# Alternating two column tiles, matmul by matmul, in the weights-times-values product of the left-over rows, and lowering its planned cost

## The chip, the cores and the metric

The kernel runs on one core of one Trainium2 chip. The metric is device time in microseconds, of the slowest core (here the only one).

## The reference

Attention with a threshold, then a gated feed-forward layer:

```python
scores = scale * (q @ k.T)                       # 8 batches, 8 heads, 576 rows, head dim 64
thresh = scores.max(-1) - tau
attn   = softmax(where(scores >= thresh, scores, -1e9))
x      = (attn @ v)  -> [4608, 512]
xn     = x / rms(x) * rms_g
out    = (silu(xn @ w_gate) * (xn @ w_val)) @ w_out     # 512 -> 1536 -> 512
```

576 rows are 4 chunks of 128 and 64 rows left over. The kernel puts the 64 left-over rows of two batches into one chunk of 128 ("virtual" chunks, four of them). Since the two halves need different values v, their weights-times-values product cannot be one matmul on all 128 output rows; it runs on two column tiles of TensorE, 64 output rows each.

## The kernel before

The product, for two head pairs `i` per block. `kind == "v"` is a virtual chunk; its two `rows` are the two column tiles. 8 such blocks run in the kernel, 64 plain ones.

```python
def fn(o):
    for i in range(2):
        w, p = wt[(s - 1 + i) % NWT], p1 - 1 + i
        rows = [(slice(0, 128), b % 2)] if kind == "m" else [(HALF[e], e) for e in range(2)]
        for rs, vi in rows:
            at = 2 * i * (D + 1)
            nc.tensor.matmul(ring[...][rs, at:at + 2 * (D + 1)], w[:, 4, rs], va[vi][:, p, 8:10], start=True, stop=False)
            for h in range(2):
                for j in range(4):
                    nc.tensor.matmul(ring[...][rs, at:at + D + 1], w[:, 5 * h + j, rs], va[vi][:, p, 2 * j + h], ...)
                at += D + 1
```

The kernel does not issue its operations in the order in which the source names them. Each is recorded with a planned cost, and a planner then decides, with a model of engines and buffers, in which order all engines get their instructions:

```python
COST = dict(s_main=932.0, s_virt=900.0, ..., av_main=310.0, av_virt=480.0, ...)   # planned ns
...
o = add("PE", 2 * COST["av_main" if kind == "m" else "av_virt"], s + AV_PRIO, deps, fn, ring="R", mode=...)
...
seq = order_ops(ops, {"R": 4})       # 4 PSUM buffers, shared by transposes, products and feed-forward
for o in seq:
    o.fn(o)
```

Scores have PSUM buffers of their own, one per head of a pair (`s_ps`); VectorE reads them (line 592), and the next score step (line 569; its 16 or 8 matmuls are called a score block below) may overwrite a half only when that has been read.

## Time and profile before

| | before |
|---|---|
| median time, 3 runs | 563.74 us (563.67 to 563.99) |
| TensorE busy | 554.2 us, 99% |
| the 8 column-tile blocks, first to last start | 942 ns each, 7.5 us in all |
| TensorE waiting seen between instructions after 98.9 us | 0.6 us |

The profiled span is 561.9 us, about 1.8 us less than the time of an execution. The prediction shows the lines and says how they are read.

### The profile page before, as it was taken

What the parts mean: (1) busy time and instruction counts of PE and PEld (TensorE: products, weight loads), DVE (VectorE), ACT (ScalarE), POOL (GpSimd) and SP (SyncE); (2) the same over time, 40 slices, a digit from 0 to 9 for tenths busy, and PEclk for the clock granted to TensorE, in tenths of its full rate; (3) what the DMA queues carried; (4) which work ended last, traced back from release to release, by engine and by line L of the source; (5) the groups of instructions that cost most, each with busy time, mean ns of one, the idle gap of its engine ahead of it and who ended that gap; (6) DMA issues with size and microseconds to landing.
All of it is one profiled execution on the core that took longest, in us unless ns stands there. A gap on an engine that the chain in (4) does not pass through costs nothing.

```text
span 561.9 us, 15217 instructions
## 1 busy us (share of the span) xinstructions
PE 554.2 (99%) x5768; PEld 316.4 (56%) x5768; DVE 425.3 (76%) x1091; ACT 460.0 (82%) x741; POOL 322.4 (57%) x462
## 2 busy tenths in 40 slices
PE   8999999999999999999999999999999999999997
PEld 4756666757667455545555455545555444445674
DVE  4989977869968589658885889578966886586354
ACT  5999999998989788879888997888988988885332
POOL 2378846975767456665667666666666664551000
PEclk9999999999999999999999999999999999999999
DMA  9999999889976499889997799989998544652211
GB/s 200 271 291 250 173 179 216 161 143 198 195 181 115 116 174 160 185 156 183 154 176 175 121 170 176 182 177 156 174 189 179 110 97 97 151 95 53 85 38 38
DMA packets 270025, 89.08 MB, mean 159 GB/s; under 512 B 252544, under 2 KB 262272, under 8 KB 269952
## 3 DMA queue, kind: packets, MB, share of 16 engines
q1 hardware_dynamic: 267168, 86.02, 76.4%
q0 software_dynamic: 1600, 1.57, 1.7%
q8 instruction: 45, 0.74, 0.6%
q10 hardware_dynamic: 1184, 0.52, 0.3%
q14 instruction: 28, 0.23, 0.1%
HBM read 37.75 MB, written 9.44 MB: 84 GB/s over the span
## 4 chain that ended last, share of the span: by engine, by line
PE 95%; DVE 2%; POOL 1%; ACT 1%; issue 1%; DVEq 0%; POOLq 0%
PE s_ps L569 29%; PE ring L795 17%; PE ring L800 16%; PE ring L865 15%; PE ring L700 6%; PE ring L304 2%; PE ring L696 2%; DVE ssb L592 1%; PE ring L662 1%; PE ring L365 1%; PE s_ps L800 1%; PE s_ps L840 1%; PE s_ps L865 1%; PE s_ps L262 1%; PE s_ps L795 0%
## 5 line engine op out<-in xcount | busy, mean ns | idle before, releaser
L592 DVE CUSTOM_DVE_ANT_0 ssb<-s_ps,zrow 128x576 f32<-128x576 f32 x288 | 207.1, 753 | 64.3 <-PE s_ps L569 46.5
L610 ACT ACTIVATE ssb<-ssb,nth 128x576 f32<-128x576 f32 x224 | 166.1, 767 | 26.7 <-POOL nth L599 26.2
L569 PE MATMUL s_ps<-qkt 64*64 64x288 f32 (+1 forms) x1792 | 166.4, 417 | 1.5 <-DVE mx L592 1.5
L643 POOL TENSOR_SCALAR wsb<-ssb,nth 128x576 f16<-128x576 f32 x64 | 110.5, 1726 | 11.6 <-DMA wt<-wsb 6.3
L795 PE MATMUL ring<-xnT,wg 128*128 128x256 f16 (+1 forms) x564 | 114.4, 325 | 0.3 <-DVE xsb L718 0.3
L569 PEld LDWEIGHTS s_ps<-qkt 64*64 64x64 f32 (+1 forms) x1792 | 78.4, 140 | 62.8 <-DVE mx L592 15.5
L800 PE MATMUL ring<-xnT,wv 128*128 128x512 f16 (+1 forms) x528 | 110.4, 331 | 0.0
L599 POOL TENSOR_SCALAR nth<-mx 128x2 f32<-128x2 f32 x144 | 31.7, 220 | 128.6 <-DVE mx L592 114.4
L812 DVE SCALAR_TENSOR_TENSOR sl<-th,ring 128x256 f32<-128x256 f32 (+1 forms) x141 | 77.0, 546 | 30.5 <-ACT th L809 29.5
L617 ACT ACTIVATE wsb<-ssb 128x1152 f16<-128x1152 f32 x80 | 93.0, 1162 | 3.4 <-DMA wt<-wsb 1.1
L809 ACT ACTIVATE th<-ring 128x256 f32<-128x256 f32 (+1 forms) x141 | 67.7, 481 | 30.7 <-PE ring L795 26.6
L865 PE MATMUL ring<-wo,hf 128*128 128x512 f16 x384 | 90.0, 380 | 0.0
L648 POOL TENSOR_TENSOR wsb<-wsb,esb 128x576 f16<-128x576 f16 x64 | 81.8, 1279 | 10.1 <-ACT esb L629 5.7
L817 DVE TENSOR_TENSOR hf<-ring,sl 128x512 f16<-128x512 f32 (+1 forms) x132 | 75.0, 568 | 9.3 <-PE ring L800 0.5
L800 PEld LDWEIGHTS <-wv 128*128 128x128 f16 x576 | 52.2, 98 | 44.5 <-issue 14.2
L795 PEld LDWEIGHTS <-wg 128*128 128x128 f16 x576 | 52.0, 98 | 42.2 <-issue 12.2
L865 PEld LDWEIGHTS <-hf 128*128 128x128 f16 x408 | 37.3, 98 | 47.0 <-issue 7.0
L629 ACT ACTIVATE esb<-ssb,nth 128x576 f16<-128x576 f32 x64 | 49.2, 769 | 6.4 <-POOL nth L599 6.0
L700 PE MATMUL ring<-va,wt 128*128 128x65 f16 (+1 forms) x1264 | 52.9, 193 | 0.0
L700 PEld LDWEIGHTS <-wt 128*128 128x128 f16 (+1 forms) x1280 | 48.7, 100 | 3.8 <-issue 0.7
L614 ACT ACTIVATE wsb<-ssb 128x576 f16<-128x576 f32 x64 | 43.6, 681 | 1.6
L696 PE MATMUL ring<-va,wt 128*128 128x130 f16 (+1 forms) x158 | 35.1, 227 | 0.6 <-ACT qTv L473 0.6
(68 smaller groups left out, 444.8 us busy)
## 6 DMA issues: line engine op xcount, KB each, us to landing
vst<-in_v_dram SPq DMA_DIRECT2D x32, 256.0 KB, 3.8
qkn<-in_k_dram SPq DMA_DIRECT2D x31, 256.0 KB, 4.5
out_dram<-osb SPq DMA_DIRECT2D x31, 256.0 KB, 2.8
qkn<-in_q_dram SPq DMA_DIRECT2D x28, 256.0 KB, 4.2
stage<-in_moe_w_gate_dram SPq DMA_DIRECT2D x6, 512.0 KB, 6.1
stage<-in_moe_w_val_dram SPq DMA_DIRECT2D x6, 512.0 KB, 6.2
wt<-wsb SPq DMA_TRANSPOSE x128, 3.2
wo<-in_moe_w_out_dram POOLq DMA_DIRECT2D x4, 384.0 KB, 6.9
```

Source lines behind the costliest of these rows:

```text
L569: nc.tensor.matmul(s_ps[h][rows, ROW_AT + n * part:ROW_AT + n * part + n], lhs(hs), kT[i][p][h][hs, n * part:n * part + n], start=True, st ...
L592: nc.vector.tensor_tensor_reduce(out=ssb[a][:, h], in0=s_ps[h][:, ROW_AT:ROW_AT + S], in1=zrow, scale=-1.0 / 8.0, scalar=3.0e38, op0=ALU.a ...
L610: nc.scalar.activation(out=ssb[a][:, h], in_=ssb[a][:, h], func=PRELU, scale=-1.0, bias=nth[m][:, h:h + 1], **PRELU_KW)
L617: nc.scalar.activation(out=wsb[s % NW], in_=ssb[a], func=AF.Exp)
L643: nc.gpsimd.tensor_scalar(out=wsb[s % NW][:, h], in0=ssb[a][:, h], scalar1=nth[m][:, h:h + 1], scalar2=None, op0=ALU.is_le)
L648: nc.gpsimd.tensor_tensor(out=wsb[s % NW][:, h], in0=wsb[s % NW][:, h], in1=esb[es], op=ALU.mult)
L700: nc.tensor.matmul(ring[o.slot[0]][rs, at:at + D + 1], w[:, 5 * h + j, rs], va[vi][:, p, 2 * j + h], start=False, stop=(h == 1 and j == 3))
L795: nc.tensor.matmul(ring[o.slot[0]][:, 0:n], wg[d][:, fs], xnT[slot][:, d, 0:n], start=(d == 0), stop=(d == 3))
L800: nc.tensor.matmul(ring[o.slot[0]][:, 0:n], wv[d][:, fs], xnT[slot][:, d, 0:n], start=(d == 0), stop=(d == 3))
L812: nc.vector.scalar_tensor_tensor(out=sl[i][:, 0:n], in0=th[i][:, 0:n], scalar=1.0, in1=ring[g.slot[0]][:, 0:n], op0=ALU.add, op1=ALU.mult)
L817: nc.vector.tensor_tensor(out=hf[hi][:, 0:n], in0=ring[vv.slot[0]][:, 0:n], in1=sl[i][:, 0:n], op=ALU.mult)
L865: nc.tensor.matmul(ring[(first or o).slot[0]], hf[hs[fc][0]][:, 128 * j:128 * (j + 1)], wo[:, fc], start=(fc == 0), stop=(fc == NFC - 1))
```

## The change

The matmuls of the two column tiles alternate one by one, so that the two tiles can work at the same time. The planned cost of such a block is lowered with it.

```diff
-    ..., av_main=310.0, av_virt=480.0, ...
+    ..., av_main=310.0, av_virt=320.0, ...
@@
+                at = 2 * i * (D + 1)
                 for rs, vi in rows:
-
-                    at = 2 * i * (D + 1)
                     nc.tensor.matmul(... w[:, 4, rs], ... start=True, stop=False)
-                    for h in range(2):
-                        for j in range(4):
+                for h in range(2):
+                    for j in range(4):
+                        for rs, vi in rows:
                             nc.tensor.matmul(... w[:, 5 * h + j, rs], ... start=False, stop=(h == 1 and j == 3))
-                        at += D + 1
+                    at += D + 1
```

More of the change, by code (lines that the diff above doesn't have):

```diff
@@ L16 @@
 COST = dict(
-    s_main=932.0, s_virt=900.0, tr_qk=530.0, tr4=230.0, tr_full=440.0, av_main=310.0, av_virt=480.0, ffn4=216.0, warm=3500.0,
+    s_main=932.0, s_virt=900.0, tr_qk=530.0, tr4=230.0, tr_full=440.0, av_main=310.0, av_virt=320.0, ffn4=216.0, warm=3500.0,
     ttr=690.0, evac_qk=600.0, evac_half=380.0, evac_kt=350.0, prelu=700.0, exp2=1250.0, exp1=690.0, exp0=690.0,
```

## The prediction

> **What bounds the kernel now**
>
> I read five views, from coarse to fine. First the head of the page, its busy times and its chain of work that ended last.
>
> ```profile
> span 561.9 us, 15217 instructions
> PE 554.2 (99%) x5768; PEld 316.4 (56%) x5768; DVE 425.3 (76%) x1091; ACT 460.0 (82%) x741; POOL 322.4 (57%) x462
> PE 95%; DVE 2%; POOL 1%; ACT 1%; issue 1%; DVEq 0%; POOLq 0%
> ```
>
> TensorE is busy 99% of the span and holds 95% of the chain. Busy alone proves little, since overlapping matmuls count as one stretch, but the chain agrees: what shortens TensorE's own work shortens the kernel, unless something else has become the limit at that place.
>
> So I asked where that might be, with busy time by stretch. The first 98.9 us hold no instruction that the change touches. The columns are the stretch, its length, then busy us with instruction counts for PE, PEld, DVE, ACT and POOL, the granted clock, the DMA share and GB/s.
>
> ```profile
> 98.90:175.00 76.10, 75.53 (x905) 51.00 (x905) 60.83 (x176) 68.50 (x118) 54.51 (x73) 1.00 0.88 171
> 175.00:520.00 345.00, 345.00 (x3455) 177.96 (x3454) 265.09 (x641) 292.50 (x455) 207.67 (x284) 1.00 0.77 149
> ```
>
> From 175 to 520 us PE is busy 345.00 of 345.00. From 98.9 to 175 us it misses 0.57 us, ACT is at 90% and DMA at 88%. That stretch hides more waiting, because a wait between two halves of a score block lies under matmuls still in flight. The chain in order of time shows it (start, length, engine and line):
>
> ```profile
> 127.95 1.13 PE s_ps L569 x16
> ...
> 133.30 1.69 PE s_ps L569 x16
> ...
> 142.04 1.70 PE s_ps L569 x16
> ```
>
> A score block of 16 matmuls takes 1.13 us undisturbed; some here take 1.69. I compared every block and gap after 98.9 us with the median of its kind: about 2.9 us of excess lies between 98.9 and 175 us (0.73 us of it before the weights-times-values block at 173.55), and 0.27 us in all the rest. So there are two regimes: some slack up to 175 us, none afterwards.
>
> Now the operations themselves. The rows by form show which of the weights-times-values matmuls are touched: those in 128*64, on one column tile.
>
> ```profile
> L700 PE MATMUL ring<-va,wt 128*128 128x65 f16 x1008 | 44.4, 193 | 0.0
> L700 PE MATMUL ring<-va,wt 128*64 128x65 f16 x256 | 8.4, 195 | 0.0
> L696 PE MATMUL ring<-va,wt 128*64 128x130 f16 x32 | 7.1, 244 | 0.0
> ```
>
> There are 256 + 32 = 288 of them, in 8 blocks of 36: two head pairs, times two batches, times one 130-wide and eight 65-wide matmuls. Do not read their cost from 8.4 and 7.1: those spans overlap each other. Nor from 195 ns, which is the latency of one. What counts is start to start, which the timeline of the first block gives (start, length, line, form, count):
>
> ```profile
> 98.92 0.24 PE L696 MATMUL ring<-va,wt 128*64 128x130 f16 x1
> 99.00 0.32 PE L700 MATMUL ring<-va,wt 128*64 128x65 f16 x5
> 99.14 0.24 PE L696 MATMUL ring<-va,wt 128*64 128x130 f16 x1
> 99.16 0.38 PE L700 MATMUL ring<-va,wt 128*64 128x65 f16 x8
> 99.35 0.24 PE L696 MATMUL ring<-va,wt 128*64 128x130 f16 x1
> 99.37 0.38 PE L700 MATMUL ring<-va,wt 128*64 128x65 f16 x8
> 99.56 0.24 PE L696 MATMUL ring<-va,wt 128*64 128x130 f16 x1
> 99.59 0.47 PE L700 MATMUL ring<-va,wt 128*64 128x65 f16 x11
> 99.99 0.71 PE L569 MATMUL s_ps<-qkt 64*64 64x288 f32 x8
> ```
>
> Each group of nine opens with one L696. The openings are 0.21 us apart, but the last group runs from 99.56 to its last matmul at 99.862, which is 0.30 us. So the groups already overlap by about 0.09 us: at 99.14 only five of the first tile's eight L700 had started.
>
> **What the Trainium skill says**
>
> "TensorEngine Tiling (Array Packing)", section Key Properties: different tiles can execute weight loads and matmuls in parallel. The trace agrees: the opening of the second tile at 99.14 comes before three matmuls of the first.
>
> "TensorE: Matmul & The Clock Gate", section Back-to-back issue gap, gives N/2.4 + 2.5 ns warm, which is an estimate of 29.6 ns for 65 columns. Inside one tile I find gaps of 28 to 36 ns, most 29 to 35, at a granted clock of 1.00: it agrees as a floor.
>
> The same page, section "The mechanism" in its Part 3, holds that matmuls start and end in strict program order. The trace before disagrees, for tiles that differ in columns: at 99.14 the tenth matmul of the program starts ahead of the seventh. This matters, as it shows a look-ahead already at work; it reaches only about three matmuls past the end of a tile.
>
> "TensorEngine Tiling (Array Packing)", section Key Properties, also says that changing the mode drains the engine. The trace: a plain matmul follows a 512-column one after 216 ns, a column-tile matmul after 309; and leaving the block costs 124 instead of 29. The change does not touch these 93 + 95 ns per block.
>
> **The change part by part**
>
> Nothing is removed or added: the same 288 matmuls and weight loads, the same evacuations. Within a head pair the two openings are now issued together and the other sixteen alternate between the tiles.
>
> Cost of a block before, first start to last start: 3 x 213 + 303 = 942 ns (measured 939 to 944 in all eight).
>
> Cost after, if each tile keeps its own pace and both run at once: within one tile the opening is followed after 81 ns, then seven gaps averaging 31.4 ns make 301 ns (98.922 to 99.223 in the trace). The second head pair starts one gap later, 30 ns. So 301 + 30 + 301 = 632, plus the offset of the second tile, about 6 ns as seen between a first-tile matmul at 99.130 and the second tile's opening at 99.136: about 640 ns. The saving is 942 - 640 = 302 ns a block, and 8 x 0.302 = 2.4 us.
>
> Which part is on the path? Six of the eight blocks (191.67, 202.49, 323.37, 330.36, 451.31 and 458.31 us) lie in the stretch without slack: 6 x 0.302 = 1.8 us, surely on the path. The two at 98.92 and 105.08 us lie before the stretch with 2.9 us of waiting, which may absorb their 0.6 us; I count about half. That makes -2.1 us.
>
> The diff has a second part, easy to overlook: the planning cost of such a block falls from 480 to 320 per head pair. No instruction has that cost, but the kernel orders its own instructions from these numbers. Comparing built orders: TensorE's blocks stand the same up to the sixth after the second of the eight, then differ; buffers, DVE, ACT and the DMA queue shift with them. Building one part of the diff at a time shows that the planning cost alone makes the whole reordering. Mode changes count 342 in both; one more score step uses four small tiles instead of two, about 60 ns by 799 + 335 against 838 + 236. The final ten output matmuls stand the same, and the streamed output stage starts one pair earlier, still five pairs behind its input. So the order adds no work that I can count. What it can do is add or take away waits of the 0.1 to 0.7 us seen above. Mean taken as 0, spread about 0.8 us.
>
> Sum: 563.74 - 2.1 = 561.6 us.
>
> **The rivals**
>
> Rival one, a shared path: if weight loads, or the streamed values, of the two tiles had to go one after the other, alternating would gain nothing, and 563.7 stays. Against it: in steady state a group of 130 + 8 x 65 = 650 columns starts every 213 ns, 3.05 columns per ns, where one tile alone manages 65 per 31.4 ns, 2.07. For it: that is 1.5 times, not yet 2 times, so a ceiling just above is not excluded. At a ceiling of 3.05 nothing is gained; I give that 12%.
>
> Rival two, the gain is used up by a wait: TensorE comes sooner to a score block whose buffer VectorE has not freed, or to weights whose transpose is still in flight. ACT at 82% and DVE at 76% over the span, and the full stretch from 175 us, speak against more than a few such. It would leave 562.5 to 563.5.
>
> Rival three, the new order is unlucky or lucky: only 2.9 us of excess is there to win after 98.9 us, so at best some 560; a bad order could cost 1 to 2 us and end at 563 to 564. The planning number now matches my 640 ns block (2 x 320), as the old one matched 942 (2 x 480 = 960), so I expect no worse planning.
>
> **Range and chances**
>
> Full overlap with everything on the path gives 561.3, with the two early blocks lost 561.9; adding the order's 0.8 us either way gives 560.4 to 562.9 for 8 in 10. A change of 2% is 11.3 us, more than the whole 8 x 0.942 = 7.5 us of these blocks, so within 2% is 0.98, with 0.01 each side.
>
> **What would show it right or wrong**
>
> Right: openings of the two tiles start some 6 ns apart and the pair repeats after about 0.33 us; first to last start of a block is 620 to 680 ns; single L700 latencies stay near 195 ns; L569 follows the block's first start by about 0.76 us instead of 1.06; PE stays at 99% and the span falls by about 2 us. Wrong on rate: a block still takes over 850 ns. Wrong on the path: blocks take 640 ns, but score blocks of 1.3 to 1.7 us, or waits, appear after 175 us and the span hardly moves. Wrong on order: the block's saving is there, and the time differs from it by over 1 us either way.

## The result

| | runs | median us | ratio to before | 95% interval |
|---|---|---|---|---|
| before | 4 | 563.87 (563.67 to 564.53) | | |
| changed | 4 | 562.97 (562.58 to 564.90) | 0.9987 | 0.9969 to 1.0005 |

A ratio is worked out from the runs of both kernels, and is not quite the ratio of the medians. Here its interval includes 1, so these four runs alone do not show a gain. The median lies just above the predicted range of 560.4 to 562.9, and well above its middle of 561.6.

The profiled execution was the slowest of the four (564.90 us); its page begins:

```profile
span 562.9 us, 15231 instructions
PE 552.9 (98%) x5776; PEld 315.4 (56%) x5776; DVE 425.6 (76%) x1091; ACT 458.9 (82%) x741; POOL 322.5 (57%) x462
PE 92%; DMA 3%; DVE 2%; ACT 1%; issue 1%; POOL 0%; DVEq 0%; POOLq 0%; ACTq 0%
```

TensorE lost 1.3 us of busy time and yet the span grew by 1.0 us. The chain of work now names DMA with 3%. The view of waits of TensorE shows one long wait that the kernel before did not have:

```profile
PE ring L695 <- DMA wt<-wsb: 1.6, 1, 1.6
```

It falls at about 87 us, where the program is still the same as before, and neither a second execution of the same kernel (e1 below) nor the runs e3, e5, e6 and e9, which keep its order up to there, have it. It belongs to that execution, not to the change.

The operations themselves did what was hoped for. The first block in the timeline (start, length, line, form, count), to be held against the one in the prediction (line 696 there is line 695 here):

```profile
101.14 0.25 PE L695 MATMUL ring<-va,wt 128*64 128x130 f16 x2
101.22 0.42 PE L700 MATMUL ring<-va,wt 128*64 128x65 f16 x16
101.48 0.22 PE L695 MATMUL ring<-va,wt 128*64 128x130 f16 x2
101.54 0.42 PE L700 MATMUL ring<-va,wt 128*64 128x65 f16 x16
101.89 0.72 PE L569 MATMUL s_ps<-qkt 64*64 64x288 f32 x8
```

The openings now come in twos (x2), the other sixteen stand in one row, and the following score step starts 0.74 us after the block's first start, where it was 1.06. First to last start is 617 to 620 ns in all eight blocks, where it was 939 to 944: 0.325 us less each, 2.6 us together. The rows by form show no longer duration of a single matmul. The profile models the ends of matmuls, so the starts above are the better evidence:

```profile
L700 PE MATMUL ring<-va,wt 128*64 128x65 f16 x256 | 5.8, 195 | 0.0
L695 PE MATMUL ring<-va,wt 128*64 128x130 f16 x32 | 3.8, 232 | 0.0
```

So 2.6 us left these blocks and, by the medians, only about 0.9 us left the kernel. Where the rest went is seen in the chain in order of time, after 175 us. In the kernel before it names a score block of over 1.20 us twice:

```profile
261.08 1.22 PE s_ps L569 x8
402.49 1.26 PE s_ps L569 x16
```

In the changed kernel it names seven (start, length, engine and line):

```profile
263.26 1.53 PE s_ps L569 x16
282.85 1.53 PE s_ps L569 x16
331.31 1.56 PE s_ps L569 x16
342.04 1.26 PE s_ps L569 x16
400.25 1.26 PE s_ps L569 x16
411.00 1.26 PE s_ps L569 x16
499.28 1.28 PE s_ps L569 x16
```

An undisturbed block of 16 takes 1.13 us. Three of these wait 0.4 us and four some 0.13 to 0.15 us. Summing over all score blocks after 175 us what first-to-last start exceeds the undisturbed 799 ns (838 for the form with large tiles) gives 0.20 us before and 1.77 us in the changed kernel. No wait is listed for these: TensorE still counts as busy with matmuls in flight.

The next view shows why, at the first of them. It is from e1, the same kernel's undisturbed execution. TensorE:

```profile
259.05 1.24 PE L569 MATMUL s_ps<-qkt 64*128 64x288 f32 x8
260.13 0.66 PE L304 MATMUL ring<-id,qkn 64*128 64x64 f32 x16
260.72 0.23 PE L695 MATMUL ring<-va,wt 128*128 128x130 f16 x1
...
261.42 1.60 PE L569 MATMUL s_ps<-qkt 64*64 64x288 f32 x16
```

and VectorE:

```profile
260.32 0.76 DVE L592 CUSTOM_DVE_ANT_0 ssb<-s_ps,zrow 128x576 f32<-128x576 f32 x1 [0.17 <-PE s_ps L569]
...
261.01 0.75 DVE L592 CUSTOM_DVE_ANT_0 ssb<-s_ps,zrow 128x576 f32<-128x576 f32 x1
261.69 0.08 DVE L592 DVE_READ_ACCUMULATOR2_ANT mx<- 128x1 f32 x1
```

The second score step starts at 261.42, only 2.37 us after the first, with short work between. VectorE reads the first step's second half until 261.77, so the half of the new step that overwrites it cannot start before. The starts of its sixteen matmuls, which the view merges, show it: one of the four tiles keeps the times of an undisturbed step (0, 0.29, 0.54 and 0.78 us after the first start), and the other three begin together 0.4 us late, at 261.83 to 261.84. In the order of the kernel before, a score step at that place had two feed-forward blocks more ahead of it and started 4.16 us behind the first (261.02 and 265.18).

### The profile page after: what moved, and what is told of

It reads as the page before. It is cut to its first block, busy times and chain, and to the rows that moved or that the text cites. A ratio compares the mean times of both kernels' runs of the same rounds, so it can differ in the third digit from the quotient of the medians.

```text
span 562.9 us, 15231 instructions
## 1 busy us (share of the span) xinstructions
PE 552.9 (98%) x5776; PEld 315.4 (56%) x5776; DVE 425.6 (76%) x1091; ACT 458.9 (82%) x741; POOL 322.5 (57%) x462
## 4 chain that ended last, share of the span: by engine, by line
PE 92%; DMA 3%; DVE 2%; ACT 1%; issue 1%; POOL 0%; DVEq 0%; POOLq 0%; ACTq 0%
PE s_ps L569 29%; PE ring L800 16%; PE ring L795 16%; PE ring L865 14%; PE ring L700 6%; DMA wt<-wsb 2%; PE ring L304 2%; PE ring L695 2%; DVE ssb L592 1%; PE ring L662 1%; DMA qkn<-in_q_dram 1%; PE s_ps L840 1%; PE s_ps L865 1%; PE ring L365 1%; PE s_ps L795 1%
## 5 line engine op out<-in xcount | busy, mean ns | idle before, releaser
L800 PE MATMUL ring<-xnT,wv 128*128 128x512 f16 (+1 forms) x548 | 112.9, 329 | 0.0
L795 PE MATMUL ring<-xnT,wg 128*128 128x512 f16 (+1 forms) x544 | 111.9, 328 | 0.3 <-DVE xsb L718 0.3
L812 DVE SCALAR_TENSOR_TENSOR sl<-th,ring 128x512 f32<-128x512 f32 (+1 forms) x136 | 75.1, 553 | 21.9 <-ACT th L809 20.7
L809 ACT ACTIVATE th<-ring 128x512 f32<-128x512 f32 (+1 forms) x136 | 65.7, 485 | 26.3 <-PE ring L795 23.3
L817 DVE TENSOR_TENSOR hf<-ring,sl 128x512 f16<-128x512 f32 (+1 forms) x137 | 76.8, 561 | 9.8
L700 PE MATMUL ring<-va,wt 128*128 128x65 f16 (+1 forms) x1264 | 50.4, 193 | 0.0
L700 PEld LDWEIGHTS <-wt 128*128 128x128 f16 (+1 forms) x1280 | 46.1, 100 | 4.3 <-issue 0.7
L695 PE MATMUL ring<-va,wt 128*128 128x130 f16 (+1 forms) x158 | 31.8, 225 | 2.4 <-DMA wt<-wsb 1.6
```

Source lines behind the costliest of these rows:

```text
L700: nc.tensor.matmul(ring[o.slot[0]][rs, at:at + D + 1], w[:, 5 * h + j, rs], va[vi][:, p, 2 * j + h], start=False, stop=(h == 1 and j == 3))
L795: nc.tensor.matmul(ring[o.slot[0]][:, 0:n], wg[d][:, fs], xnT[slot][:, d, 0:n], start=(d == 0), stop=(d == 3))
L800: nc.tensor.matmul(ring[o.slot[0]][:, 0:n], wv[d][:, fs], xnT[slot][:, d, 0:n], start=(d == 0), stop=(d == 3))
L812: nc.vector.scalar_tensor_tensor(out=sl[i][:, 0:n], in0=th[i][:, 0:n], scalar=1.0, in1=ring[g.slot[0]][:, 0:n], op0=ALU.add, op1=ALU.mult)
L817: nc.vector.tensor_tensor(out=hf[hi][:, 0:n], in0=ring[vv.slot[0]][:, 0:n], in1=sl[i][:, 0:n], op=ALU.mult)
```

## The experiments

Two theories were on the table. A: alternation saves its 2.3 to 2.6 us, and the new order, which comes from the planned cost alone, costs over 1 us. B: the saving is swallowed by waits whatever the order. C was a side theory: that the transpose wait at 87 us belongs to the change.

Runs with an interval, each against the kernel before on the same chip.

| run | column tiles | planned cost | median us | ratio | 95% interval |
|---|---|---|---|---|---|
| e1 | alternate | 320 (the change) | 563.10 | 0.9981 | 0.9966 to 0.9996 |
| e2 | alternate | 480 (as before) | 561.70 | 0.9959 | 0.9947 to 0.9972 |
| e3 | one, then the other | 320 | 565.48 | 1.0023 | 1.0010 to 1.0037 |
| e4 | alternate | 360 | 562.11 | 0.9964 | 0.9951 to 0.9976 |
| e7 | alternate | 400, scores 1000 | 564.16 | 0.9998 | 0.9985 to 1.0010 |
| e8 | alternate | 400, scores 1000, maximum 790 | 571.45 | 1.0132 | 1.0117 to 1.0148 |
| e9 | alternate | 320, three steps moved | 564.37 | 1.0003 | 0.9990 to 1.0017 |
| e10 | alternate | 440 | 560.43 | 0.9933 | 0.9921 to 0.9946 |
| e11 | alternate | 440, one step moved | 560.85 | 0.9942 | 0.9928 to 0.9956 |
| e12 | one, then the other | 440 | 563.43 | 0.9983 | 0.9953 to 1.0013 |

The median of the kernel before was 563.99 us beside e1 to e8, 564.22 beside e9 to e11 and 564.69 beside e12; these three groups ran on different chips, so compare ratios between them.

### e1: the change once more

No edit.

> The changed kernel once more, unaltered, because its profiled run was the slowest of its four (564.9 us against 562.6 to 563.1) and waited 1.8 us for a weight transpose before 98.9 us, where the program is the same as before. Theory A (alternation saves 2.6 us, the new order gives back about 1.3): 562.7 us, ratio to the kernel before near 0.998, blocks 617 ns, about 1.5 us more score-block waiting after 175 us than the kernel before. Rival B (the saving is swallowed by waits whatever the order): the same time, so this run alone does not separate them. Rival C (the transpose wait at 87 us belongs to the change): it comes back here, and the time stays above 563.5.

563.10 us, ratio 0.9981. The first column-tile block starts at 99.37 us instead of 101.14, and the wait for a transpose at 87 us is gone. Theory C is out. The change gains about 0.2%, with an interval just clear of zero.

### e2: alternation alone

```diff
-    av_virt=320.0
+    av_virt=480.0
```

With the old number every engine gets its instructions in the order of the kernel before, except for the alternation itself.

> Alternation alone: the planning cost put back to 480, so that all engines' instructions stand as in the kernel before. Theory A (the order gave the gain back): blocks of 617 ns, 8 x 0.325 = 2.6 us saved, score-block waiting after 175 us back near 0.3 us: 561.3 us; 561.6 if the two early blocks are absorbed. Rival B (absorbed whatever the order): 562.8 us, like the whole change, with blocks of 617 ns and new waits. Rival C: like A without any change in waits, but 561.3 in the whole change's good runs too, which e1 would show.

561.70 us, 2.3 us under the kernel before. The blocks take 616 to 619 ns (one 726). Rival B expected 562.8 and is out. Dividing the trace at the third block shows where it is gained: from the first block's start to the third's start 92.48 us against 92.75, so 0.27 us of the 0.65 us of the two early blocks; from there to the last matmul 364.66 against 366.20, 1.55 us of the 1.95 us of the other six. The rest is in score blocks after 175 us, 0.61 us of excess against 0.20. From the first block on that makes 1.8 us. The profiled execution was the slowest of e2 (562.53 us), so its trace does not show where the other 0.5 us of the medians' 2.3 us lie.

### e3: the planned cost alone

The kernel before, with

```diff
-    av_virt=480.0
+    av_virt=320.0
```

> The planning cost alone: 320 as in the change, so its order on every engine, but each column tile whole, as before. Theory A: blocks stay at 942 ns, score blocks placed too close behind the previous one wait as in the changed kernel (about 1.0 us more than before; the wait beside a column-tile block at 331 us shrinks by the longer block): 564.9 us, slower than before by 1.0. Rival B: the order is neutral, 563.9 us. If the order were a gain in itself: under 563.5.

565.48 us, 1.5 us slower than the kernel before, where 1.0 was expected. The column-tile blocks take 939 to 945 ns, as before, and no other usual distance between matmuls grew (medians by kind, after 98.9 us). From the first block's start to the last matmul e3 takes 1.34 us more than the kernel before (460.29 against 458.95), and its score blocks after 175 us exceed by 1.64 us, against 0.20. So the order alone costs about what the change had lost, and the two parts add up: +1.5 and -2.3 are -0.8, and e1 shows -0.9.

### e4: a third order

```diff
-    av_virt=320.0
+    av_virt=360.0
```

Here a rule was tried that would tell a good order before it runs. In the traces of both kernels, most score steps that start 2.84 us or more behind the previous one wait for nothing, and those at 2.20, 2.37 and 2.64 us wait about 0.56, 0.40 and 0.13 us: the wait is about what is missing to 2.76 us. Such shortfalls can be summed from the built order and the block durations of the traces (an estimate).

> Alternation with planning cost 360 in place of 320: a third order. From the built order and block durations of the traces, score steps starting less than 2.76 us after the previous one sum to 2.7 us of shortfall after the second column-tile block, against 3.8 in the changed kernel and 2.6 in the kernel before. Theory A with this spacing rule: 1.1 us under the changed kernel, 561.7 us. Rival B: 562.8 us like the changed kernel. Spacing rule wrong but order matters: anything else outside 0.5 us of 561.7.

562.11 us: 1.0 us under e1 in the same rounds, where 1.1 was expected. Score blocks after 175 us exceed by 0.94 us, against 2.07 in e1.

### e5 and e6: how near the two tiles must stand

Both keep the order of the change on all other work. e5 alternates in runs of four, e6 issues the two openings together and then eight of one tile and eight of the other. The edit of e5:

```diff
 for h in range(2):
-    for j in range(4):
-        for rs, vi in rows:
+    for rs, vi in rows:
+        for j in range(4):
```

> The changed kernel, with the two column tiles alternating in runs of four matmuls instead of one by one (same planning cost, so the same order on all other work). If TensorE starts a matmul of the other tile up to about three places ahead of its turn, as the kernel before shows at each end of a tile, runs of four are within that reach: a block near 617 ns as with strict alternation, at most 660. If two matmuls overlap only when they are neighbours in the program, three of four lose their partner: 800 ns or more.

> The changed kernel, with the two 130-wide openings of a head pair together but then eight matmuls of one tile followed by eight of the other. A look-ahead of three places: the second tile starts its eight when the first has three left, so a block of about 765 ns, between 617 and 942. If the gain came from the openings alone: near 617. If neighbours alone overlap: 900 or more.

Blocks of e5 take 643 to 646 ns, of e6 826 to 831 (single looks at 563.49 and 565.28 us). So the second tile's matmuls need not be neighbours of the first's: four places apart costs 26 ns more than alternating. With eights the block is between both ends, as a short look-ahead would have it, but 60 ns longer than my estimate of 765. The first block of e6 in the timeline shows the order of starts:

```profile
98.98 0.25 PE L695 MATMUL ring<-va,wt 128*64 128x130 f16 x2
99.06 0.48 PE L700 MATMUL ring<-va,wt 128*64 128x65 f16 x13
99.35 0.24 PE L695 MATMUL ring<-va,wt 128*64 128x130 f16 x1
99.37 0.28 PE L700 MATMUL ring<-va,wt 128*64 128x65 f16 x5
99.47 0.22 PE L695 MATMUL ring<-va,wt 128*64 128x130 f16 x1
```

The opening of the next head pair starts at 99.35 when thirteen of the sixteen before it have started, so it too runs three places ahead, and the second opening comes only at 99.47: the pair no longer stands together. My estimate had not followed that.

### e7 and e8: orders picked and spurned by the rule

More planned numbers were changed, the cost of score steps for e7 and that of the maximum step too for e8:

```diff
-    s_main=932.0, s_virt=900.0, av_virt=320.0, ttr=690.0
+    s_main=1000.0, s_virt=1000.0, av_virt=400.0, ttr=690.0      # e7
+    s_main=1000.0, s_virt=1000.0, av_virt=400.0, ttr=790.0      # e8
```

> Alternation with planning numbers 400 for a column-tile head pair and 1000 for both kinds of score steps (932 and 900 before): an order picked because its built sequence has few score steps less than 2.76 us behind the previous one. Shortfall after the second column-tile block 1.0 us, against 3.8 in the changed kernel, and TensorE's own work by block durations 1.7 us less (fewer switches between kinds). Spacing rule right: up to 4.5 us under the changed kernel, so 558.5 to 560.0 us, the best of all. If spacing is not what costs (the order's loss has another source), or other waits come in its place: 561.5 to 564.

> Alternation with planning numbers 400, 1000 for both kinds of score steps and 790 for the maximum step (690 before): picked for a bad sequence. Shortfall of spacing after the second column-tile block 6.2 us against 3.8 in the changed kernel, TensorE's own work 1.1 us less. Spacing rule right: about 1.3 us over the changed kernel, near 564.3 us, with score blocks of up to 2.5 us. Spacing rule wrong: it ends with e7 or with the changed kernel, 562.9 or less.

Both miss. e7 was to be the best and ended at 564.16 us, level with the kernel before. These numbers change the plan from the very start, and my sum only judged the part after the second column-tile block. In the first 98.5 us TensorE is busy 93.18 us in e7 and 94.21 in e1, so about 1 us more is lost there. In the part that was judged, the sum of 1.0 us was too small as well: score blocks after 175 us alone exceed by 1.97 us. Where the rest of the miss lies stays open. e8 went the expected way and far past the expected 564.3: 571.45 us. Its view of waits has something that the rule does not count at all:

```profile
PE ring L662 <- ACT wsb L617: 4.3, 4, 1.6
```

These are transposes on TensorE waiting for ScalarE's exponentials. Its score blocks after 175 us exceed by 3.92 us, too. The rule is thus no planner: it ignores every wait but one.

### e9: moving the three crowded steps

A few lines after the planner let the three score steps that waited 0.4 us in the changed kernel change places with the feed-forward block that follows each. Nothing else moves.

```diff
-    seq = order_ops(ops, {"R": 4})
+    seq = spaced(order_ops(ops, {"R": 4}))     # in three places: [score step, feed-forward] -> [feed-forward, score step]
```

> The changed kernel with one surgical edit of its order: the three score steps that waited 0.40, 0.40 and 0.43 us after 175 us (each behind a score step of two large tiles, then transposes, then a weights-times-values block) change places with the feed-forward block that follows them; all else stands as in the changed kernel. Spacing theory: those waits vanish, two smaller ones of about 0.07 us appear behind, one more switch between kinds costs about 0.09: 0.9 to 1.1 us under the changed kernel, ratio to the kernel before about 0.9965, near 562.0 us. If the lost time has another source, such as the rest of the new order, the waits move elsewhere and the time stays at 562.9, ratio 0.998.

It got slower: 564.37 us, ratio 1.0003 against 0.9981. The two intervals overlap a little, but the traces decide. The three waits of the score steps are gone, and the feed-forward blocks in their places wait longer. The first place in the timeline (the wait before a row stands in brackets):

```profile
260.25 0.41 PE L700 MATMUL ring<-va,wt 128*128 128x65 f16 x8
261.12 1.02 PE L800 MATMUL ring<-xnT,wv 128*128 128x512 f16 x4 [0.47 <-ACT qkt L315]
262.08 1.20 PE L569 MATMUL s_ps<-qkt 64*64 64x288 f32 x16
```

and the waits of TensorE after 175 us:

```profile
PE ring L800 <- DVE xsb L718: 0.9, 1, 0.9
PE ring L795 <- ACT qkt L315: 0.8, 1, 0.8
PE ring L800 <- ACT qkt L315: 0.5, 1, 0.5
```

A feed-forward block needs one of the four PSUM buffers. The transposes hold two and the product one, until ScalarE and VectorE have copied them out. By the gap before it, such a block starts 0.64, 1.05 and 0.90 us late, where the score step had lost 0.40, 0.40 and 0.43: 2.6 us in place of 1.2. So the place itself is crowded: a score step, transposes and a product in a row leave more to evacuate than there is time for, and swapping the neighbour only picks which buffer TensorE waits for. The planner had picked the cheaper one.

### e10, e11 and e12: the best order found, with and without alternation

e10 is the changed kernel with another planned cost, e11 is e10 with one step moved as in e9, and e12 is the kernel before with the same planned cost. The edit of e10:

```diff
-    av_virt=320.0
+    av_virt=440.0
```

> Alternation with planning cost 440: a fourth order, unchanged up to 98.9 us unlike the two replanned ones that missed. Shortfall of spacing after the second column-tile block 1.9 us, against 2.6 for planning cost 480 and 3.8 for 320; TensorE's own work 0.15 us more than either. Spacing rule: 0.5 us under alternation with the old plan, 561.2 us, ratio about 0.995. If the rule fails again: anywhere from 561.7 to 564.

> The kernel with planning cost 440 and one of its crowded score steps (0.40 us short) behind the feed-forward block that follows it. Spacing rule: 0.3 us less, about 560.9 us, the best of all; a difference this small may not stand out of the noise of some 0.2 us.

> Planning cost 440 without alternation: the order of the fastest kernel so far, each column tile whole. If the two parts add up (alternation 2.3 to 2.6 us, this order about 1.2 us better than the old plan's): 562.8 us, ratio 0.9975 to 0.998. If this order is good only because the blocks in it are short: 564 or more. If the order alone makes the gain: under 561.5.

e10, alternation with 440, ends at 560.43 us and beats both kernels: ratio 0.9933, 3.8 us under the median before. It was expected at 561.2. Its advantage over e2 lies early: between 98.9 and 175 us its score blocks exceed by 1.2 us, against 2.8 in e2 and 2.5 in the kernel before, and after 175 us by 0.78, against 0.61 in e2. So the stretch that the prediction called slack is where this order gains. e11 moves one of its crowded steps as e9 did, and again does not gain (560.85 us), as its feed-forward block now starts 0.53 us late where the step had lost 0.40. e12, the same order without alternation, has ratio 0.9983: the order is worth about 0.2% and alternation about 0.5% in it. e12 alone does not show the 0.2%, as its interval includes 1 (two of its six runs and two of the eleven beside it were over 1.6 us above their medians); under alternation the intervals of e2 and e10 do not overlap. Alternation was worth 0.41% in the old order (e2) and 0.42% in the new (e3 to e1), so its value hardly depends on the order.

## Why the prediction was wrong, by its own steps

**The bound.** Right. TensorE's own work shortened and the kernel with it, as far as the order was held still (e2).

**The saving per block.** Right in mechanism and nearly in size: 302 ns were expected from 942 to 640, and 325 were measured, to 617. The tiles' offset is 2 to 5 ns and the opening of a tile is followed sooner in the second head pair (after 55 to 58 ns instead of 81), which I had not foreseen. One reading beside it was off: the prediction calls 29.6 ns a floor for the gaps inside a tile, though it counts gaps of 28 itself. The section of the Trainium skill that it cites ("TensorE: Matmul & The Clock Gate", Back-to-back issue gap) gives the formula for isolated matmuls and says that at small sizes it under-counts where each matmul has its weight load, as here; the mean gap of 31.4 ns is only 1.8 ns more. The saving rests on that mean, not on the formula.

**Which part is on the path.** Right in the main. About half of the 0.6 us of the two early blocks was to be lost and 0.38 of 0.65 was (e2). The six late ones were to be "surely on the path", and 1.55 of their 1.95 us was: 0.4 us came back as waits of score blocks. By time, e2 gained 2.3 us where 2.1 were predicted; its trace shows 1.8 from the first block on. So the near match is partly luck: the blocks shrank more than expected, and less of it reached the end.

**The order.** This is the step that failed: "Mean taken as 0, spread about 0.8 us", with "so I expect no worse planning". The new order costs 1.5 us by itself (e3). I had counted what an order adds in work (switches between kinds, forms of score steps) and found nothing. That holds as far as the trace of e3 shows: its blocks take no longer, and it loses in score blocks that wait for VectorE, 1.64 us after 175 us against 0.20. I had the block durations and the built order, and the chain in order of time of the kernel before already showed that a score step can take 1.69 us instead of 1.13; comparing distances between score steps in both orders would have shown 3.8 us of shortfall against 2.6, thus the sign and about the size here, though the same sum failed for e7 and e8. The argument that a truer number plans better did not hold either: 320 is close to the measured block (617 ns and one gap, over two head pairs, is 323) and made the worst of the four orders that differ in this number alone; 440 made the best.

**The rivals.** Rival one, a shared path that leaves no gain, is out: two tiles stream 36 matmuls in 617 ns, where the prediction works out 632 for the 18 of one. Rival two, the gain used up by waits whatever the order, is out by e2. Rival three, an unlucky order that ends at 563 to 564, is what happened, at the low end, since the forecast of alternation was a little too small. The range was too narrow because it gave the order 0.8 us; the orders tried here, relative to the old one under alternation, came to +1.4 (e1), +0.4 (e4), -1.5 (e10, each against its own rounds), and +2.5 and +9.8 where more numbers changed (e7, e8).

**What stays open.** That the planned cost's order costs 1.5 us is shown; that the loss sits in score blocks close behind others is read from the traces, and no run took these waits away while all else stood. What would make these places cheaper is not: moving the score step did not (e9, e11). Nor did I find a rule that foretells an order's time: the spacing sum was off by 0.1 us for e4 (1.0 against 1.1 under e1) and by 1.0 for e10 (1.5 against 0.5 under e2), but by over 4 us for e7 and e8.

## What to carry to other kernels

When a change also alters a number from which instructions are ordered, measure the two apart: here they were worth -2.3 and +1.5 us, and the sum alone would have sold the idea short. Do not judge a new order by counting its work: the distances between steps that share a buffer show where it may wait. They do not replace a run, as e7 and e8 show. Expect a swap at a crowded place to move the wait to another buffer. Issue the work for two column tiles within a few places of each other: a block took 617 ns when they alternated, 643 in runs of four and 826 in runs of eight.

## What the Trainium skill lacked or had wrong

- "TensorE: Matmul & The Clock Gate", "The mechanism" in Part 3: it has matmuls start and end in strict program order. For two column tiles the kernel before starts the second tile's opening (99.14 us) ahead of the first tile's last three matmuls. The issue overhead of about 4 ns a tile, in the next section there ("Measured speedup vs the span model"), agrees with the 2 to 5 ns between tiles here.
- How far this look-ahead reaches for matmuls stands on no page. These runs: blocks of 617 ns when tiles alternate, 643 to 646 in runs of four, 826 to 831 with openings together and then eights, 939 to 945 with whole tiles of nine.
- "TensorEngine Tiling (Array Packing)", Key Properties: a change of mode drains the engine, and the page names no cost for it. Here entering the column tiles costs 93 ns more than a plain matmul (309 against 216 ns), and leaving 95 ns more (124 against 29).
